# Signs of float64 weights from a leaky rectifier's slope, and weights measured in two groups, in an attention and two-MLP kernel

## The chip, the cores and the metric

One core of one Trainium2 chip runs the whole program. The metric is the device time of one execution in microseconds (us); less is better. TensorE (PE) multiplies, VectorE (DVE) and ScalarE (ACT) prepare its operands and empty PSUM, SyncE (SP) issues the DMAs.

## The reference

```python
x = attention(q, k, v)         # 4 batches, 8 heads, 576 tokens, head size 64, mask in blocks of 64
h = x @ w_in                   # 2304 x 512 times 512 x 2048
x = np.maximum(0.01 * h, h) @ w_out
h = x @ w2_in                  # the second MLP, of the same sizes
return (h * (1.0 / (1.0 + np.exp(-h)))) @ w2_out
```

The weights of both MLPs come as 64-bit floats; q, k and v as 32-bit floats.

## The kernel before

The kernel writes all work down as tasks with a rank and planned costs; a planner (`Schedule.run`) then fixes one order per engine, and on the chip each engine works through its own list and waits at each instruction until its inputs are there. So a change of a cost or a rank reorders everything around it.

The 2304 tokens are cut into six blocks of 384. Block 0's attention comes first. Then the first MLP runs block by block, and its 2048 inner columns in 16 slices, each a step: H (the first product, into the one bank `h`), the gate on ScalarE (leaky rectifier from `h` to `g`), `ghi` (ScalarE) and `glo` (VectorE), its two 16-bit halves, and A (the second product, into `acc` and `u`). PE's list is H of a step, A of the step before, H of the next step, so a gate has an A's time to free `h`. Block 0 multiplies in 32 bits (lines 1763 and 1789), blocks 1 to 5 with two 16-bit halves of x, of the gate and of the weights (lines 1768 to 1770 and 1797). The attention of block n + 1 is laid among the steps of block n: scores `s<-k,q` (lines 1369 and 1462) go into two PSUM banks, the row maximum is DVE's, exp (`p`, line 1480) ACT's, the halves of p ACT's and DVE's (1494, 1499); a DMA transposes them and PE weighs v with them (1312).

The weights are made in three stages.

- `convert` turns 64-bit floats into 32-bit ones, 128x512 at a time: 32 tiles of the first MLP while block 0 is at work, 32 of the second later. Line 441 loads `raw` (three buffers). Line 449 (ACT) scales the upper word as if it were a 32-bit float, so that three zero bits stand ahead. Line 461 (DVE, or 457 on ACT) puts the three low bits that belong to the number into the lower half of a word of `cc`; line 466 (DVE) puts the sign bit into its upper half. Line 479 (DVE) shifts the scaled word left by three, which drops its sign, and joins it with `cc`.
- `measure_weights` (line 530, ACT) and `range_of_weights` find one power of two for all 32 tiles: a maximum, a DMA transpose across partitions (559) and small DVE instructions (550 to 579).
- `split_weights` makes each tile's two 16-bit halves: high (line 614, ACT) and low (line 619, DVE). Block 1's step needs those of its slice.

The gate of blocks 1 to 5 (line 1826) scales by the constant `DOWN`; `w_back` brings the output of a block back. The second MLP works on pairs of blocks in 32 bits (2044 to 2046), then in 16 bits (2223), with sums of products on DVE (2069 to 2080).

Of the kernel before, what the change touches and what calls it, by code (L numbers as in the profile page):

```python
# [7 lines left out]
F32 = mybir.dt.float32  # L8
# [55 lines left out]
V_SLOTS = ((16, 17, 18, 19), (20, 21, 25, 26))  # L64
SPLIT_LEAD, W_RANK, VB_LEAD = 55.0, 0.4, 4.0

# [178 lines left out]
def attn_mlp_mlp(  # L245
# [183 lines left out]

    def convert(src, f, sl, rk, load_rank, to=None, slow=0, lag=0, joint=False, free=()):  # L430

        d = {}
        raw_free, raw_after, raw_users = raws.next()
        cy_free, cy_after, cy_users = cys.next()
        cc_free, cc_after, cc_users = ccs.next()

        def load():
            r = raw_room().bitcast(I64)  # L440
            nc.sync.dma_start(out=r, in_=src[f, :, sl])
            d["r"] = r.bitcast(F32)
            d["w0"] = r.bitcast(U32).rearrange("p (n two) -> p n two", two=2)[:, :, 0]
            d["sign"] = r.bitcast(U16).rearrange("p (n four) -> p n four", four=4)[:, :, 3]
# [6 lines left out]
        def half_words(i):  # L451
            return d["c"].bitcast(U16).rearrange("p (n two) -> p n two", two=2)[:, :, i]

        def low(e):
            d["c"] = cc_room(U32)
            if e == "ACT" and joint:
                nc.scalar.activation(half_words(0), d["w0"], AF.Copy, scale=LOW, bias=-0.5)
            elif e == "ACT":
                nc.scalar.activation(half_words(0), d["w0"], AF.Copy, scale=2.0**-29)
            elif joint:  # L460
                nc.vector.tensor_scalar(half_words(0), d["w0"], 2.0**-29, -0.50001, op0=ALU.mult, op1=ALU.add)
            else:
                nc.vector.tensor_scalar(half_words(0), d["w0"], 2.0**-29, None, op0=ALU.mult)
# [4 lines left out]
        def shifted(e):  # L468
            yu = d["y"].bitcast(U32)
            nc.vector.tensor_scalar(yu, yu, 3, None, op0=ALU.logical_shift_left)  # L470

        def added(e):
            ci = d["c"].bitcast(I32)
            d["x"] = d["c"].bitcast(F32) if to is None else to()
            engine[e].tensor_tensor(d["x"].bitcast(I32), d["y"].bitcast(I32), ci, op=ALU.add)
# [15 lines left out]
        if joint:  # L491
            t_x = plan.add({"DVE": dve(DM)}, [t_y, t_w, t_c, *free], rk, joined)
        else:
            t_t = plan.add({"DVE": dve2x(DM) + 60}, [t_y], rk, shifted)
            t_x = plan.add({"DVE": dve(DM) + 70}, [t_w, t_c, t_t], rk, added)
        raw_users += [t_y, t_w, t_c]
# [14 lines left out]
    def first_weights():  # L511

        got = []
        for i in range(2 * NF):
            f, sl = i // 2, slice((i % 2) * DM, (i % 2 + 1) * DM)
            rk = CONV0 + CONV1 * f
            to = lambda f=f, sl=sl: wx[f][:, sl]
            got.append(convert(w1, f, sl, rk, LOAD0 + RAW0 + 20 * i if i < 4 else rk - CONV_LOAD, to, slow=LATER if i < 4 else 0, joint=True))
        return got

    def measure_weights():

        t_zero = plan.add({"POOL": 150}, [], -100, lambda e: nc.gpsimd.memset(w_sums, V_LEAST))
        tasks = []
        for i, (d, t_x, _) in enumerate(w1_got):
            at = i % 2 * (2 * NF + 1) + i // 2

            def sized(e, d=d, at=at):
                if e == "ACT":
                    nc.scalar.activation(  # L530
                        w_junk, d["x"], AF.Square, scale=SQUARE, accum_out=w_sums[:, at : at + 1]
                    )
                else:
                    nc.vector.tensor_reduce(
                        w_sums[:, at + NF : at + NF + 1], d["x"], axis=AX.X, op=ALU.max, apply_absolute_value=True
                    )

            tasks.append(plan.add({"ACT": act(DM) + 200, "DVE": dve(DM)}, [t_x, t_zero], CONV0 + CONV1 * (i // 2) + W_RANK, sized))
        return tasks

    def range_of_weights():

        sums = w_sums.rearrange("p (s f) -> p s f", s=2)
        top, half, mult, back = (w_small[:, 2 * i : 2 * i + 2] for i in range(4))
        tops = w_tops.rearrange("p (s q) -> p s q", s=2)
        rk = -100.0

        def squared(e):
            m = sums[:, :, NF : 2 * NF]
            nc.vector.scalar_tensor_tensor(m, m, 4 * SQUARE**2, m, op0=ALU.mult, op1=ALU.mult)  # L550
# [27 lines left out]
        def both_back(e):  # L578
            nc.vector.scalar_tensor_tensor(
                w_back, back[:, 0:1], 1.0 / DOWN, back[:, 1:2], op0=ALU.mult, op1=ALU.mult  # L580
            )

        t = plan.add({"DVE": 190}, measure_weights(), rk, squared)
        t = plan.add({"DVE": 200}, [t], rk, most)
        ts = [plan.add({"ACT": act(P), "DVE": 170}, [t], rk, lambda e, s=s: spread(e, s)) for s in (0, 1)]
        t = dma(ts, -1000.0, 80640, turned, 1200, lag=PT_LAG)
        t = plan.add({"DVE": dve(2 * P) + 90}, [t], rk, topped)
        t_half = plan.add({"DVE": 160}, [t], rk, halved)
# [3 lines left out]
        w1_range.update(mult=mult, t_mult=t_mult, t_back=plan.add({"DVE": 160}, [t], 0, both_back))  # L592

    w1_range = {}

    def split_weights():
# [3 lines left out]
        for i in range(2 * NF):  # L600
            f, side = i // 2, i % 2
            sl = slice(side * DM, (side + 1) * DM)
            d, t_x, _ = w1_got[i]
            by = w1_range["mult"][:, side : side + 1]

# [16 lines left out]

            deps = [t_x, w1_range["t_mult"]]
            if f in slot_of("xw"):
# [111 lines left out]
    def first_pair(p):  # L736

        rk = unit3(0, p) - W2_AHEAD
        d0, t0, users0 = convert(w2, 2 * p, slice(0, DM), rk, rk - CONV_LOAD, lag=LAG, joint=True)
        d1, t1, users1 = convert(w2, 2 * p + 1, slice(0, DM), rk, rk - CONV_LOAD, lag=LAG, joint=True)  # L740
        t_free, t_after, t_users = cys.next()
# [33 lines left out]
    def last_raw(p, rk):  # L775
# [5 lines left out]
            convert(  # L781
                w2, 2 * p + i, slice(DM, 2 * DM), rk, rk - CONV_LOAD / 4, room[i], lag=LAG, joint=True, free=busy
            ) for i in (0, 1)
# [1028 lines left out]
    def add_step(blk, f):  # L1812
# [35 lines left out]
        free = older.g_users if older else []  # L1848
        s.t_gate1 = plan.add({"ACT": act(n, True)}, [s.t_g1, *free], GATE + rk, gate1)
        s.g_users = []  # L1850
# [585 lines left out]
```

## Time and profile before

| | |
|---|---|
| time, median of 3 runs | 891.86 us (891.21 to 892.37) |
| the profiled execution | 891.37 us |
| its span, first to last instruction | 889.6 us |
| busy: PE, DVE, ACT | 866.6, 765.1, 633.7 us |
| mean granted clock of PE | 0.993 of 2.4 GHz |

A row of the profile gives a line of the kernel, the engine, the operation and its tiles (out<-in, buffer numbers left out); x is the number of instructions. Idle time stands with its releaser, the instruction whose end let the waiting one go.

### The profile page before, as it was taken

Reading aid. Unit: us, or ns where it says so; the run is one execution under the profiler, and the core shown is the slowest. Engines: PE = TensorE matmul, PEld = TensorE weight load, DVE = VectorE, ACT = ScalarE, POOL = GpSimd, SP = SyncE. Lnnn points to the kernel's source line nnn. Section 1 sums busy time; section 2 is a strip of 40 time slices with the busy share of each in tenths; the row PEclk is TensorE's granted clock in tenths of the full one; section 3 lists DMA queues with packets and bytes.
Section 4 is the critical chain, followed back from the end, with each engine's and each line's share of the span. In section 5 each row is a group of like instructions: output and inputs, shape, how many; then the busy total and the mean of one; then the engine's idle time right before and its main releaser. Section 6 shows DMA issues by size and latency. Waiting matters only on the chain.

```text
span 889.6 us, 18360 instructions
## 1 busy us (share of the span) xinstructions
PE 866.6 (97%) x6569; PEld 650.4 (73%) x6569; DVE 765.1 (86%) x1730; ACT 633.7 (71%) x1455; POOL 15.3 (2%) x75
## 2 busy tenths in 40 slices
PE   9899999998999999999999999999999989999997
PEld 4555556665676666666666668999999978888886
DVE  6888889999988998788847679989897999999976
ACT  6989889886776677677646468988797985444432
POOL 0000000000000000000000000000000000000000
PEclk9999999998999999999999999999999999999999
DMA  8579838765668589655535226588868874553531
GB/s 288 180 212 221 233 105 216 185 132 131 166 150 164 133 172 196 150 144 113 110 65 185 93 71 227 195 289 267 277 205 269 287 253 141 157 163 121 165 108 60
DMA packets 179179, 155.71 MB, mean 175 GB/s; under 512 B 108304, under 2 KB 155152, under 8 KB 179088
## 3 DMA queue, kind: packets, MB, share of 16 engines
q1 hardware_dynamic: 179088, 154.54, 62.2%
q8 instruction: 51, 0.84, 0.4%
q14 instruction: 40, 0.33, 0.1%
HBM read 93.85 MB, written 35.65 MB: 146 GB/s over the span
## 4 chain that ended last, share of the span: by engine, by line
PE 68%; DVE 9%; ACT 4%; DMA 2%; issue 2%; SPq 0%; DVEq 0%; POOL 0%; ACTq 0%; POOLq 0%
PE acc L1797 11%; PE acc L2223 7%; PE h L1768 5%; PE h L1770 5%; PE h L1769 5%; PE s L2223 5%; PE s L1462 4%; PE u L1797 4%; PE x L1312 2%; PE u L2223 2%; PE x L2223 2%; PE acc L2045 2%; PE acc L2044 2%; PE acc L2046 2%; PE s L2044 1%
## 5 line engine op out<-in xcount | busy, mean ns | idle before, releaser
L1797 PEld LDWEIGHTS <-w 128*128 128x128 f16 x840 | 78.6, 98 | 54.6 <-issue 4.4
L1797 PE MATMUL acc<-ghi,w 128*128 128x384 f16 x420 | 103.1, 328 | 0.8 <-ACT cc L1901 0.8
L1768 PE MATMUL h<-h,w 128*128 128x384 f16 x280 | 92.6, 331 | 0.8 <-DVE w L619 0.8
L1769 PE MATMUL h<-l,w 128*128 128x384 f16 x280 | 92.1, 329 | 0.0
L1770 PE MATMUL h<-h,w 128*128 128x384 f16 x280 | 92.1, 329 | 0.0
L1480 ACT ACTIVATE p<-s,st 128x288 f32<-128x288 f32 (+4 forms) x120 | 62.4, 521 | 40.1 <-DVE st L1472 24.7
L1462 PE MATMUL s<-k,q 128*128 128x288 f32 (+5 forms) x288 | 77.5, 364 | 5.3 <-ACT p L1480 5.1
L1826 ACT ACTIVATE g<-h 128x384 f32<-128x384 f32 x80 | 39.1, 489 | 48.6 <-PE h L1770 47.9
L412 DVE TENSOR_TENSOR glo<-g,ghi 128x384 f16<-128x384 f32 x80 | 44.3, 554 | 28.9 <-ACT ghi L401 28.0
L1797 PE MATMUL acc<-glo,w 128*128 128x384 f16 x210 | 68.5, 326 | 0.0
L1494 ACT ACTIVATE hl<-p,st 128x576 f16<-128x576 f32 (+5 forms) x90 | 55.0, 626 | 17.9 <-issue 6.7
L1499 DVE SCALAR_TENSOR_TENSOR hl<-p,st,hl 128x576 f16<-128x576 f32 (+4 forms) x96 | 58.8, 625 | 3.3 <-ACT hl L1494 2.8
L1462 PEld LDWEIGHTS s<-k,q 128*128 128x128 f32 x288 | 46.9, 190 | 18.6 <-ACT p L1480 8.7
L2223 PEld LDWEIGHTS <-y 128*128 128x128 f16 x525 | 51.8, 99 | 10.6 <-issue 3.0
L2223 PEld LDWEIGHTS <-x 128*128 128x128 f16 x492 | 48.3, 98 | 6.1 <-issue 0.3
L2105 ACT ACTIVATE h<-e 128x384 f32<-128x384 f32 x96 | 46.9, 489 | 1.8
L2096 ACT ACTIVATE e<-e 128x384 f32<-128x384 f32 (+1 forms) x72 | 42.2, 621 | 6.0 <-DVE e L2076 6.0
L449 ACT ACTIVATE cy<-raw 128x512 f32<-128x512 f32 x64 | 42.5, 667 | 3.1 <-DMA raw<-w 2.9
L1768 PEld LDWEIGHTS <-w 128*128 128x128 f16 x280 | 27.5, 98 | 21.7 <-issue 3.1
L401 ACT ACTIVATE ghi<-g 128x384 f16<-128x384 f32 x77 | 40.2, 522 | 1.4
L1770 PEld LDWEIGHTS <-w 128*128 128x128 f16 x280 | 27.6, 99 | 18.5 <-issue 0.7
L1769 PEld LDWEIGHTS <-w 128*128 128x128 f16 x280 | 27.7, 99 | 15.4 <-issue 0.7
(347 smaller groups left out, 2367.6 us busy)
## 6 DMA issues: line engine op xcount, KB each, us to landing
raw<-w SPq DMA_DIRECT2D x64, 512.0 KB, 4.8
raw<-g SPq DMA_DIRECT2D x64, 256.0 KB, 3.2
g<-e SPq DMA_DIRECT2D x48, 192.0 KB, 3.4
g<-e SPq DMA_DIRECT2D x24, 384.0 KB, 2.9
kqr<-kq_l SPq DMA_DIRECT2D x16, 480.0 KB, 3.7
kqr<-kq_l SPq DMA_DIRECT2D x16, 416.0 KB, 3.4
y<-yT SPq DMA_DIRECT2D x12, 384.0 KB, 4.7
l<-w2k SPq DMA_DIRECT2D x18, 256.0 KB, 4.3
```

Of the source, the lines that this page charges most:

```text
L412: engine[e].tensor_tensor(lo, x, hi, op=ALU.subtract)
L449: nc.scalar.activation(d["y"], d["top"], AF.Copy, scale=2.0**-112)
L1462: nc.tensor.matmul(s[:, :w], hd.q[:, a : a + P], hd.k[:, k0:k1], start=i + j == 0, stop=i == len(hds) - 1 and j == 1,)
L1480: nc.scalar.activation(p[:rows, k0:k1], u.s[piece][:rows, :w], AF.Exp, bias=nm[:rows], accum_out=s2[:rows, piece : piece + 1])
L1494: nc.scalar.activation(hl[:rows, 0, :n], p[:rows], AF.Copy, scale=rc[:rows])
L1499: nc.vector.scalar_tensor_tensor(hl[:rows, 1, :n], p[:rows], rc[:rows], hl[:rows, 0, :n], op0=ALU.mult, op1=ALU.subtract)
L1768: nc.tensor.matmul(h, w1_lo[s.f][:, sl], hi[:, c, : s.n], start=c == 0, stop=False)
L1769: nc.tensor.matmul(h, w1_hi[s.f][:, sl], lo[:, c, : s.n], start=False, stop=False)
L1770: nc.tensor.matmul(h, w1_hi[s.f][:, sl], hi[:, c, : s.n], start=False, stop=c == NC - 1)
L1797: nc.tensor.matmul(s.acc[c][:, : s.n], a, b, start=s.f == 0 and i == 0, stop=s.f == NF - 1 and i == 2)
L2105: nc.scalar.activation(h_all[:, :n], out_()[:, at : at + n], AF.Square, scale=SQUARE, accum_out=sum_at(col))
L2223: nc.tensor.matmul(o, a[:, x], b, start=i == 0 and j == 0 and q == 0, stop=i == NP - 1 and q == 2, skip_group_check=True,)
```

## The change

The weights' conversion no longer has a sign instruction: line 449 becomes a leaky rectifier with slope 2^32 for negative numbers, whose larger exponent becomes the sign bit when line 479 shifts left by three. The low bits become a full 32-bit word: a shift on DVE, or a scaled copy on ACT.

The weights are measured, scaled and split in two groups, slices 0 to 5 and 6 to 15, each with a power of two of its own. The gate's constant scale becomes a column of `w_downs`, one number per partition, that makes up for the group's power of two. Four planning numbers move: conversions rank earlier (CONV0), measuring earlier (W_RANK), the attention of blocks 2 to 5 earlier (ATT), and splits 11 steps later (SPLIT_LEAD), which puts them behind whatever else is ready.

```diff
-CONV0, CONV1, CONV_LOAD = 10.5, 0.7, 78.0
-ATT0, ATT1, ATT, ATT_SLOPE, AHEAD, V_LATE = 11.0, 0.3, 54.0, 0.8, 7.5, 0.0
+CONV0, CONV1, CONV_LOAD = 9.0, 0.7, 78.0
+ATT0, ATT1, ATT, ATT_SLOPE, AHEAD, V_LATE = 11.0, 0.3, 44.0, 0.8, 7.5, 0.0
-SPLIT_LEAD, W_RANK, VB_LEAD = 55.0, 0.4, 4.0
+W_GROUPS = ((0, 6), (6, 16))
+SPLIT_LEAD, W_RANK, VB_LEAD = 66.0, -3.0, 4.0
...
         def scaled(e):
             d["y"] = cy.tile([P, DM], F32, tag="cy", name="cy")
-            nc.scalar.activation(d["y"], d["top"], AF.Copy, scale=2.0**-112)
+            nc.scalar.activation(d["y"], d["top"], AF.Prelu, alpha=2.0**32, scale=2.0**-112)
...
-                nc.vector.tensor_scalar(half_words(0), d["w0"], 2.0**-29, -0.50001, op0=ALU.mult, op1=ALU.add)
+                nc.vector.tensor_scalar(d["c"], d["w0"], 29, None, op0=ALU.logical_shift_right)
-        def signed(e):
-            nc.vector.tensor_scalar(half_words(1), d["sign"], 0x8000, None, op0=ALU.bitwise_and)
...
-        t_c = plan.add({"DVE": dve2x(DM) + 110}, [t_load], rk, signed, [t_w])
+        t_x = plan.add({"DVE": dve(DM)}, [t_y, t_w, *free], rk, joined)
+        raw_users += [t_y, t_w]
...
+        n = len(W_GROUPS)
+        for g in range(n):
+            range_of_group(g)
+        most, factor = w_small[:, 8 * n : 8 * n + 1], w_small[:, 8 * n + 1 : 8 * n + 2]
+        def largest(e):
+            nc.vector.tensor_reduce(most, w_backs, axis=AX.X, op=ALU.max)
+        def inverse(e):
+            nc.vector.tensor_scalar(factor.bitcast(I32), most.bitcast(I32), EXPONENT, None, op0=ALU.bitwise_xor)
+        def downs(e):
+            nc.vector.tensor_scalar(w_downs, w_backs, factor, 0.5 * DOWN, op0=ALU.mult, op1=ALU.mult)
+        def whole_back(e):
+            nc.vector.tensor_scalar(w_back, most, 1.0 / DOWN, None, op0=ALU.mult)
...
-                nc.scalar.activation(s.g, s.h[:, :n], AF.Prelu, alpha=LEAK, scale=DOWN)
+                at = group_of(f)
+                nc.scalar.activation(s.g, s.h[:, :n], AF.Prelu, alpha=LEAK, scale=w_downs[:, at : at + 1])
```

On DVE, in block 0, the conversion of two tiles stands before as follows (479 joins, 466 makes the sign, 461 the low bits, 1380 and 1381 belong to the attention).

```order
L479 SCALAR_TENSOR_TENSOR x<-cy,cc 128x512
L466 TENSOR_SCALAR cc<-raw 128x512
L461 TENSOR_SCALAR cc<-raw 128x512
L479 SCALAR_TENSOR_TENSOR x<-cy,cc 128x512
L466 TENSOR_SCALAR cc<-raw 128x512
L1380 TENSOR_SCALAR st<-st 128x2
L1381 RECIPROCAL st<-st 128x2
L479 SCALAR_TENSOR_TENSOR x<-cy,cc 128x512
```

The same place in the changed kernel (456 makes the low bits, 460 joins, 1408 is the attention's low half of p):

```order
L1390 TENSOR_REDUCE st<-s 128x1
L1408 SCALAR_TENSOR_TENSOR hl<-p,st,hl 128x256
L456 TENSOR_SCALAR cc<-raw 128x512 x2
L1408 SCALAR_TENSOR_TENSOR hl<-p,st,hl 128x256
L460 SCALAR_TENSOR_TENSOR x<-cy,cc 128x512 x2
L456 TENSOR_SCALAR cc<-raw 128x512
```

Two instructions of DVE per tile are left of three.

On DVE, between `glo` of slices 13 and 14 of block 1, the list before still holds low halves of the weights of slices 14 and 15 (`w_1727`, `w_1750`), between the attention's instructions:

```order
L412 TENSOR_TENSOR glo<-g,ghi 128x384
L619 SCALAR_TENSOR_TENSOR w_1727<-l,wm,w_1727 128x512
L1470 MEMSET s 64x64
L1472 TENSOR_REDUCE st<-s 128x1
L1499 SCALAR_TENSOR_TENSOR hl<-p,st,hl 128x576
L1474 TENSOR_REDUCE st<-s 128x1
L619 SCALAR_TENSOR_TENSOR w_1727<-l,wm,w_1727 128x512
L619 SCALAR_TENSOR_TENSOR w_1750<-l,wm,w_1750 128x512
```

In the changed kernel none is left behind slice 9's gate; the list between `glo` of slices 10 and 11 is:

```order
L413 TENSOR_TENSOR glo<-g,ghi 128x384
L1516 SCALAR_TENSOR_TENSOR hl<-p,st,hl 128x576
L1516 SCALAR_TENSOR_TENSOR hl<-p,st,hl 128x320
L1516 SCALAR_TENSOR_TENSOR hl<-p,st,hl 128x448
L1504 TENSOR_TENSOR st<-st 128x1
L1506 TENSOR_SCALAR st<-st 128x1
L1507 RECIPROCAL st<-st 128x1
L1487 MEMSET s 64x64
L1489 TENSOR_REDUCE st<-s 128x1
L413 TENSOR_TENSOR glo<-g,ghi 128x384
```

The splits have moved ahead: before, 8 of the 32 low halves stand ahead of block 1's first `glo` and 24 behind; now 21 and 11. Of the high halves on ACT, 10 stand ahead of block 1's first gate before and 27 now.

On PE, before, between A of block 1's slice 11 (`w_1549`) and H of slice 13 (`w_1657`) five pairs of scores and 72 products with v stand with no layer step among them:

```order
L1797 MATMUL u<-glo,w_1549 128x384
L1462 MATMUL s<-k,q 128x320 x2
L1462 MATMUL s<-k,q 128x448 x2
L1312 LDWEIGHTS vp
...
L1312 MATMUL x<-raw,vp 64x128
L1462 MATMUL s<-k,q 128x288 x4
L1312 LDWEIGHTS vp
...
L1462 MATMUL s<-k,q 128x512 x2
L1768 LDWEIGHTS w_1657
L1768 MATMUL h<-h_242,w_1657 128x384
```

In the changed kernel there, around H of slice 12 (`w_1385`), each pair of scores has products of a step or of v on either side:

```order
L1479 MATMUL s<-k,q 128x320 x2
L1814 LDWEIGHTS xw
L1814 MATMUL acc<-ghi,xw 128x384
...
L1329 MATMUL x<-raw,vp 64x128
L1479 MATMUL s<-k,q 128x448 x2
L1785 LDWEIGHTS w_1385
L1785 MATMUL h<-h_243,w_1385 128x384
...
L1787 MATMUL h<-h_243,w_1385 128x384
L1479 MATMUL s<-k,q 128x288 x2
L1785 LDWEIGHTS w_1385
```

The pairs of scores have been drawn apart; the number of PE's matmuls is the same in both kernels. Both kernels load ACT's function tables twice.

## Rows read from the trace of the kernel before

**Rows 1.** The page: busy time, and PE in 40 equal slices.

```profile
PE 866.6 (97%) x6569; PEld 650.4 (73%) x6569; DVE 765.1 (86%) x1730; ACT 633.7 (71%) x1455; POOL 15.3 (2%) x75
PE   9899999998999999999999999999999989999997
```

**Rows 2.** Stages: busy us per engine, PEclk, DMA share, GB/s.

```profile
40.00:140.00 100.00, 98.25 (x466) 57.04 (x465) 86.65 (x249) 87.04 (x223) 0.76 (x4) 1.00 0.72 192
140.00:198.00 58.00, 57.95 (x469) 36.49 (x469) 56.38 (x142) 50.43 (x114) 4.60 (x19) 1.00 0.79 180
198.00:205.00 7.00, 4.65 (x83) 3.05 (x81) 6.65 (x22) 5.30 (x15) 0.20 (x1) 0.98 0.44 102
205.00:212.00 7.00, 5.67 (x18) 2.66 (x19) 6.03 (x15) 3.29 (x10) 0.41 (x2) 0.53 0.75 150
```

**Rows 3.** What PE waited for: us in total, times, longest us.

```profile
PE s L1462 <- ACT p L1480: 5.1, 6, 1.7
PE s L2223 <- DVE e L2069: 2.7, 1, 2.7
```

**Rows 4.** Timeline of PE in the burst and just behind it.

```profile
205.51 1.22 PE L1462 MATMUL s<-k,q 128*128 128x512 f32 x2 [1.51 <-ACT p L1480]
207.55 0.50 PE L1768 MATMUL h<-h,w 128*128 128x384 f16 x1 [0.82 <-DVE w L619]
207.84 0.53 PE L1769 MATMUL h<-l,w 128*128 128x384 f16 x1
208.16 0.53 PE L1770 MATMUL h<-h,w 128*128 128x384 f16 x1
...
214.94 0.33 PE L1769 MATMUL h<-l,w 128*128 128x384 f16 x1
215.10 0.33 PE L1770 MATMUL h<-h,w 128*128 128x384 f16 x1
```

**Rows 5.** Timeline of PE at the end of block 0.

```profile
123.59 0.56 PE L1462 MATMUL s<-k,q 128*128 128x320 f32 x2 [1.75 <-ACT p L1480]
```

**Rows 6.** Groups of DVE: busy us, mean ns of one, idle before.

```profile
L466 DVE TENSOR_SCALAR cc<-raw 128x512 uint16<-128x512 uint16 x64 | 28.9, 455 | 0.0
L461 DVE TENSOR_SCALAR cc<-raw 128x512 uint16<-128x512 uint32 x47 | 21.5, 457 | 2.6 <-DMA raw<-w 2.4
L479 DVE SCALAR_TENSOR_TENSOR l<-cy,cc 128x512 uint32<-128x512 uint32 x20 | 13.7, 684 | 1.8 <-ACT cy L449 1.5
```

**Rows 7.** Groups of ACT, with the same columns.

```profile
L449 ACT ACTIVATE cy<-raw 128x512 f32<-128x512 f32 x64 | 42.5, 667 | 3.1 <-DMA raw<-w 2.9
L1826 ACT ACTIVATE g<-h 128x384 f32<-128x384 f32 x80 | 39.1, 489 | 48.6 <-PE h L1770 47.9
L401 ACT ACTIVATE s<-x 128x384 f32<-128x384 f32 x20 | 9.7, 486 | 12.6 <-PE x L2046 12.5
L1901 ACT ACTIVATE cc<-acc,yb 128x384 f32<-128x384 f32 x6 | 3.5, 578 | 2.3 <-DVE y L1903 1.4 <-PE acc L1797 0.9
```

**Rows 8.** The weights' instructions: ns min/median/max, first and last start in us.

```profile
L614 ACT ACTIVATE w<-w,wm x6: 728/736/748, 149.9 to 160.8; 128x512 f16<-128x512 f32 x6
L619 DVE SCALAR_TENSOR_TENSOR w<-w,wm,w x6: 731/738/747, 175.9 to 208.3; 128x512 f16<-128x512 f32 x6
L576 DVE TENSOR_SCALAR wm<-wm x1: 160/160/160, 129.3 to 129.3; 128x2 f32<-128x2 f32 x1
```

**Rows 9.** What SP's queue waited for in the first 150 us.

```profile
SPq L441 <- DVE cc L466: 29.5, 12, 10.7
```

**Rows 10.** The chain that ended last, where the second MLP starts and changes stage: start, us.

```profile
534.53 0.72 DVE cc L466 x2
...
716.35 0.88 DVE e L2069
```

**Rows 11.** Timelines of ACT and PE in a step without attention.

```profile
499.78 0.49 ACT L1826 ACTIVATE g<-h 128x384 f32<-128x384 f32 x1 [0.96 <-PE h L1770]
...
501.53 0.33 PE L1768 MATMUL h<-h,w 128*128 128x384 f16 x1
```

More of the change, by code (lines that the diff above doesn't have):

```diff
@@ L428, in attn_mlp_mlp, with convert @@
     raws, cys, ccs = Turns(RAWS), Turns(CYS), Turns(CCS)
[L430 removed]
+    def convert(src, f, sl, rk, load_rank, to=None, slow=0, lag=0, free=()):
         d = {}
@@ L448, in scaled @@
             d["y"] = cy.tile([P, DM], F32, tag="cy", name="cy")
-            nc.scalar.activation(d["y"], d["top"], AF.Copy, scale=2.0**-112)
-        def half_words(i):
-            return d["c"].bitcast(U16).rearrange("p (n two) -> p n two", two=2)[:, :, i]
+            nc.scalar.activation(d["y"], d["top"], AF.Prelu, alpha=2.0**32, scale=2.0**-112)
         def low(e):
             d["c"] = cc_room(U32)
[L456 to L460, printed above, removed]
-                nc.vector.tensor_scalar(half_words(0), d["w0"], 2.0**-29, -0.50001, op0=ALU.mult, op1=ALU.add)
-            else:
-                nc.vector.tensor_scalar(half_words(0), d["w0"], 2.0**-29, None, op0=ALU.mult)
-        def signed(e):
-            nc.vector.tensor_scalar(half_words(1), d["sign"], 0x8000, None, op0=ALU.bitwise_and)
[L468 to L475, printed above, removed]
+            if e == "ACT":
+                nc.scalar.activation(d["c"], d["w0"], AF.Copy, scale=LOW, bias=-0.5)
+            else:
+                nc.vector.tensor_scalar(d["c"], d["w0"], 29, None, op0=ALU.logical_shift_right)
         def joined(e):
@@ new lines, in sums_of, with measure_weights, sized @@
+    def sums_of(g):
+        a, b = W_GROUPS[g]
+        at = 2 * (2 * a + g)
+        return w_sums[:, at : at + 2 * (2 * (b - a) + 1)].rearrange("p (s f) -> p s f", s=2)
+    def measure_weights(g):
+        a, b = W_GROUPS[g]
+        tasks = []
+        for i in range(2 * a, 2 * b):
+            d, t_x, _ = w1_got[i]
+            sums = sums_of(g)[:, i % 2]
+            one, other = (sums[:, at : at + 1] for at in (i // 2 - a, i // 2 - a + b - a))
+            def sized(e, d=d, one=one, other=other):
@@ L539, in measure_weights @@
-        return tasks
-    def range_of_weights():
-        sums = w_sums.rearrange("p (s f) -> p s f", s=2)
-        top, half, mult, back = (w_small[:, 2 * i : 2 * i + 2] for i in range(4))
+                    nc.scalar.activation(w_junk, d["x"], AF.Square, scale=SQUARE, accum_out=one)
+                else:
+                    nc.vector.tensor_reduce(other, d["x"], axis=AX.X, op=ALU.max, apply_absolute_value=True)
+            tasks.append(plan.add({"ACT": act(DM) + 200, "DVE": dve(DM)}, [t_x, w1_range["zero"]], CONV0 + CONV1 * (i // 2) + W_RANK, sized))
@@ L545, in range_of_weights, with range_of_group @@
+        return tasks
+    def range_of_group(g):
+        a, b = W_GROUPS[g]
+        sums, small = sums_of(g), w_small[:, 8 * g : 8 * g + 8]
+        top, half, mult, back = (small[:, 2 * i : 2 * i + 2] for i in range(4))
         tops = w_tops.rearrange("p (s q) -> p s q", s=2)
+        before = w1_range.get(g - 1)
         rk = -100.0
         def squared(e):
-            m = sums[:, :, NF : 2 * NF]
+            m = sums[:, :, b - a : 2 * (b - a)]
             nc.vector.scalar_tensor_tensor(m, m, 4 * SQUARE**2, m, op0=ALU.mult, op1=ALU.mult)
@@ L579, in both_back @@
             nc.vector.scalar_tensor_tensor(
-                w_back, back[:, 0:1], 1.0 / DOWN, back[:, 1:2], op0=ALU.mult, op1=ALU.mult
+                w_backs[:, g : g + 1], back[:, 0:1], 1.0, back[:, 1:2], op0=ALU.mult, op1=ALU.mult
             )
-        t = plan.add({"DVE": 190}, measure_weights(), rk, squared)
+        t = plan.add({"DVE": 190}, measure_weights(g), rk, squared)
         t = plan.add({"DVE": 200}, [t], rk, most)
[L585 to L588, printed above, removed]
+        free = [before["turn"]] if before else []
+        ts = [plan.add({"ACT": act(P), "DVE": 170}, [t, *free], rk, lambda e, s=s: spread(e, s)) for s in (0, 1)]
+        free = [before["topped"]] if before else []
+        t_turn = dma([*ts, *free], -1000.0, 80640, turned, 1200, lag=PT_LAG)
+        t_top = plan.add({"DVE": dve(2 * P) + 90}, [t_turn], rk, topped)
+        t_half = plan.add({"DVE": 160}, [t_top], rk, halved)
         t = plan.add({"DVE": 130}, [t_half], rk, inverted)
@@ L591, in range_of_weights @@
         t = plan.add({"DVE": 130}, [t_half], 0, turned_back)
-        w1_range.update(mult=mult, t_mult=t_mult, t_back=plan.add({"DVE": 160}, [t], 0, both_back))
+        t = plan.add({"DVE": 160}, [t], 0, both_back)
+        w1_range[g] = {"mult": mult, "t_mult": t_mult, "turn": t_turn, "topped": t_top, "back": t}
+    def range_of_weights():
+        w1_range["zero"] = plan.add({"POOL": 150}, [], -100, lambda e: nc.gpsimd.memset(w_sums, V_LEAST))
+        n = len(W_GROUPS)
[10 more added lines that the diff above has]
+            nc.vector.tensor_scalar(w_back, most, 1.0 / DOWN, None, op0=ALU.mult)
+        t_most = plan.add({"DVE": 160}, [w1_range[g]["back"] for g in range(n)], 0, largest)
+        t = plan.add({"DVE": 130}, [t_most], 0, inverse)
+        w1_range["downs"] = plan.add({"DVE": 160}, [t], 0, downs)
+        w1_range["t_back"] = plan.add({"DVE": 130}, [t_most], 0, whole_back)
     w1_range = {}
@@ L603, in split_weights @@
             d, t_x, _ = w1_got[i]
-            by = w1_range["mult"][:, side : side + 1]
+            one = w1_range[group_of(f)]
+            by = one["mult"][:, side : side + 1]
             def parts(f=f, sl=sl):
@@ L621, in low @@
                 )
-            deps = [t_x, w1_range["t_mult"]]
+            deps = [t_x, one["t_mult"]]
             if f in slot_of("xw"):
@@ L781, in last_raw @@
             convert(
-                w2, 2 * p + i, slice(DM, 2 * DM), rk, rk - CONV_LOAD / 4, room[i], lag=LAG, joint=True, free=busy
+                w2, 2 * p + i, slice(DM, 2 * DM), rk, rk - CONV_LOAD / 4, room[i], lag=LAG, free=busy
             ) for i in (0, 1)
@@ L1848, in add_step @@
         free = older.g_users if older else []
-        s.t_gate1 = plan.add({"ACT": act(n, True)}, [s.t_g1, *free], GATE + rk, gate1)
+        s.t_gate1 = plan.add(
+            {"ACT": act(n, True, min(blk, 1))}, [s.t_g1, *free, *([w1_range["downs"]] if blk else [])], GATE + rk, gate1
+        )
         s.g_users = []
```

35 lines of the change are left out of this document (10 added, 25 removed).

## The prediction

> **What bounds the kernel now.** I read the busy line of the page first. PE is busy for 866.6 of a span of 889.6 us, DVE for 765.1, ACT for 633.7 [rows 1]. So 23 us of PE's time are idle, and since the change leaves the number of PE's matmuls as it is, those 23 us and the stretches of lower clock are all that it can win. Next come the 40 slices of PE: each is 22.2 us, and besides the last only three fall under 90%: the second (22 to 44 us), the tenth (200 to 222 us) and the thirty-third (711 to 734 us) [rows 1]. The windows show what these are. From 40 to 140 us, while block 0 runs and the weights are converted, PE is busy for 98.25 of 100 us, DVE for 86.65 and ACT for 87.04; from 140 to 198 us PE idles for 0.05 us. Then come 198 to 205 us with PE busy for 4.65 of 7 us, and 205 to 212 us with 5.67 of 7 and a granted clock of 0.53 [rows 2]. The waits name the partners: PE's scores wait for ACT's exp `p`, 6 times and 5.1 us in all, and one wait of 2.7 us on DVE's `e` stands in the second MLP [rows 3]. The timeline shows one place for most of this: a pair of scores that starts at 205.51 after a wait of 1.51 us, the layer's first product at 207.55 after 0.82 us on DVE's low half of a weight [rows 4]; and one wait of 1.75 us on `p` at 123.59 [rows 5].
>
> The tenth slice is a burst. PE's list holds five pairs of scores and the products with v between A of slice 11 and H of slice 13, with no layer step among them. Scores have two banks, each freed by an exp, so PE goes at ACT's and DVE's pace there, while DVE, busy for 6.65 of the first 7 us [rows 2], still has low halves of weights between the attention's instructions: the last ones run at 208.3 us [rows 8].
>
> **The change part by part.**
>
> *The sign instruction goes.* 64 times 455 ns are 28.9 us of DVE [rows 6]. PE waits for DVE in few of the places where it stood. In block 0 (32 of the 64, 14.6 us) PE has 1.75 us idle in 100 [rows 2], so nearly all of it is work that PE covers; it buys room on DVE, which the splits then use. SP's queue waited 29.5 us, 12 times, for the sign instruction to free a `raw` buffer [rows 9]; now the low bits or the scaled copy free it. That starts loads earlier, but DMA has 0.72 to 0.79 of its time taken there and PE does not wait for these loads, so I take 0.
>
> *The scaled copy becomes a leaky rectifier.* The gate is one with 128x384 at 489 ns, and a plain copy of the same size from PSUM takes 486 [rows 7]: the function costs nothing. 64 copies stay at 667 ns.
>
> *The low bits as a 32-bit shift.* No row has this instruction. Its bounds are 455 to 457 ns (one source, 16-bit output) and 684 ns (two sources, 32-bit output) [rows 6]. It has one source, so I take 457; the other end costs 0.23 us for each of the 52 that DVE now has, 27 of them ahead of block 1: 6.2 us there. On this the Trainium skill, "VectorE: DVE Perf Modes", section "What auto-detection actually checks", says that what counts is the kind of operand and the even layout, with all in SBUF: by it a single-source instruction on 32-bit words still has the faster mode. No run shown has the case; by the page the term would be the lower end.
>
> *The gate's scale from a column.* An ACT instruction with a per-partition operand of the same size took 578 ns against 486 for one without [rows 7]: 92 ns more, and 80 gates make 7.4 us of ACT. PE's next H needs `h` free, and has an A's time for that: a gate that starts at 499.78 ends at 500.27, H starts at 501.53 [rows 11]. 1.26 us of cover against 0.09, so 0; without the cover it would be the whole 7.4.
>
> *Two groups.* A second range chain is some 14 small DVE instructions at 160 ns or less [rows 8], 2.2 us, ahead of block 1, plus a DMA. All splits of slices 0 to 5 can start when 12 of the 32 tiles are measured. I count what now stands ahead of block 1's first step. On DVE: 32 signs go (−14.6), 13 more low halves of splits at 738 ns (+9.6), 2 high halves and 2 more low bits (+2.4), the range (+2.2), and some attention (+4): about +4 us net. On ACT: 17 more high halves at 736 ns (+12.5), a measurement and two low bits fewer (−2), attention that has moved behind (−5): about +5 us. Idle there are 13.35 us of DVE and 12.96 us of ACT in 40 to 140 us [rows 2]. So it fits, with 8 to 9 us left on each; but these engines' idle time lies where it lies, and new small waits of PE are to be expected. Nothing prices them but the row that they resemble, 1.75 us once [rows 5]; I put +1.0 us, from 0 to 1.75 times four for the bad case.
>
> *What the packing gives back.* The gain lies behind, in the steps of block 1: 13 low halves fewer (9.6 us of DVE) and 17 high ones fewer on ACT, and the scores drawn apart. The terms, with bounds:
> - The burst: 2.35 us idle from 198 to 205, 1.33 from 205 to 212 [rows 2], and the low clock. Behind it the layer's products start 0.32 us apart (207.84, 208.16), while at full clock it is 0.16 (214.94, 215.10) [rows 4]; of the 18 in the window some 12 are such, 1.9 us. The pair with 512 columns took 1.22 us [rows 4], where 0.56 for 320 columns [rows 5] makes 0.90: 0.3. Together 5.9; bounds 0 and 5.9. In the new list each pair of scores has layer products or products with v beside it, which cover its exp. I take 5.0, because a pair or two will still wait.
> - The end of block 0, 1.75 us [rows 5]: 0 to 1.75, take 0.9, since its `p` stands behind work of ACT that is now different.
> - The start of the second MLP: the chain goes through two signs, 0.72 us [rows 10]: 0 to 0.72, take 0.5.
> - The second MLP's change of stage: PE waits 2.7 us for `e` [rows 3], which the chain has on DVE [rows 10]. DVE's list there is the same but for one small instruction that moves ahead; signs are long done. 0 to 2.7, take 0.4.
> - The start, 22 to 44 us, where the slice shows 80 to 89% [rows 1], 2.2 to 4.4 us idle: measurements come earlier and compete on ACT, a sign less on DVE. From −1.5 to +1.5, take 0.
>
> Sum: −5.0 − 0.9 − 0.5 − 0.4 + 1.0 = −5.8 us against the profiled execution's 891.37: 885.6. The median of the runs is 0.5 above that execution, so 886.0.
>
> **The rivals.**
>
> *A, more than that.* Every named wait goes: 5.9 + 1.75 + 0.7 + 2.7 = 11.1 us, and no new one comes: 880.8. Against it: the wait in the second MLP has nothing to do with what is changed.
>
> *B, the change does not show.* PE is at 97% and the relief of DVE and ACT falls where PE covers it; the attention of the next blocks, which ranks earlier, forms its burst at another place. Then only the 0.5 to 1 us of the second MLP's start and of block 0's end is left: 890.5 to 892. For it: the attention of a block needs the same exps in the same 16 steps. Against it: from 140 to 198 us PE idles for 0.05 us in 58 with the same kind of work between the steps [rows 2], so spread work does hide.
>
> *C, slower.* The splits and the second range are packed into block 0. If the shift takes 684 ns, DVE's room of 13.35 us [rows 2] shrinks by 4 + 6.2 to 3 us, and exp's maxima and the halves of `p` come late; PE's scores then wait as they do at 205.51. Its price is that burst's, 5.9 us each time, clock included. It decides when the new waits exceed the gains and the 1.8 us of measurement: 5.0 + 0.9 + 0.5 + 0.4 + 1.8 = 8.6 us, so one burst and two waits as in [rows 5] do (5.9 + 3.5 = 9.4): 891.86 − 6.8 + 9.4 = 894.5; two bursts, 11.8, make 896.9. The row behind the burst shows what waiting costs twice: a granted clock of 0.53 from 205 to 212 us [rows 2], after a stretch with PE at 4.65 of 7. The Trainium skill, "TensorE: Matmul & The Clock Gate", section "HAM oscillation — how this bites in real kernels", describes this: an engine that is starved again and again loses its clock and pays for each stall a second time. By that, with this row, packed work that starves PE in several places would cost more than its idle time; the trace agrees for this one burst.
>
> **How the numbers follow.** The forecast (883.5 to 888.5, that is the burst gone wholly or by two thirds) has 0.55; A 0.10; B 0.18; C 0.17. A change of 0.2%, 1.8 us, is about what can be told from no change, so 890.1 to 893.6 is "same". Faster: 0.55 + 0.10 + 0.05 of B = 0.70; same 0.13; slower 0.17. The range leaves out most of C and half of A: 880.5 to 893.5.
>
> **What would show it.** In the profile after: no DVE instruction with a 16-bit output of the sign; the shift at about 457 ns, if 684 then C's condition is there; the gate at about 580 ns with H's start unmoved; the copy with the rectifier at 667. PE's tenth slice at 9, windows at 195 to 215 us with PE over 95% and a clock of 1.0; waits of scores on `p` down from 5.1 us to under 2; DVE's busy time down by some 25 us and ACT's up by 4 to 8. The steps of the second MLP shift by the same 5 us and the wait on `e` stays near 2.7. I would be wrong if the windows from 40 to 140 us show more than 3 us of idle PE, or if another window with a low clock stands where the earlier attention now ranks, in the later half of blocks 1 to 4.

## The result, and the profile after

The changed kernel takes 877.38 us, the median of four runs (876.53 to 878.52), against 891.54 for the kernel before: a ratio of 0.9844, with an interval of 0.9826 to 0.9863, that is 12 to 16 us less. The forecast was 886.0, its range 880.5 to 893.5: the direction is right, the size is not. The profiled execution after took 878.52 us, the longest of the four, with a span of 876.8, 12.8 us under that of before.

The page after, its busy line and the 40 slices of PE and of its clock:

```profile
PE 860.7 (98%) x6569; PEld 648.6 (74%) x6569; DVE 751.4 (86%) x1700; ACT 623.8 (71%) x1434; POOL 14.9 (2%) x75
...
PE   8899999999999999999999999999999999999997
...
PEclk9999999999999999999999999999999999999999
```

The tenth slice and the thirty-third, which stood at 8 in [rows 1], are at 9; the start has become no better. PE's idle time fell from 23.0 to 16.1 us, and its busy time by 5.9 us with the same number of matmuls. The windows of [rows 2], after:

```profile
40.00:140.00 100.00, 99.84 (x475) 57.79 (x474) 91.92 (x255) 91.58 (x228) 0.76 (x4) 1.00 0.77 208
140.00:198.00 58.00, 57.69 (x515) 36.81 (x515) 55.52 (x154) 42.31 (x105) 4.34 (x20) 1.00 0.72 154
198.00:205.00 7.00, 7.00 (x59) 4.37 (x54) 6.66 (x19) 6.26 (x15) 0.20 (x1) 1.00 0.74 156
205.00:212.00 7.00, 7.00 (x75) 4.57 (x74) 6.83 (x17) 3.80 (x9) 0.20 (x1) 1.00 0.76 178
```

Block 0 is fuller, by 5.3 us on DVE and 4.5 on ACT, and PE idles for 0.16 us there in place of 1.75. The burst is gone, and the clock of 0.53 with it. All that PE waits for from 40 to 300 us after (us in total, times, longest):

```profile
PE s L1479 <- ACT p L1497: 0.2, 1, 0.2
PE s L1386 <- ACT p L1394: 0.2, 1, 0.2
```

The new instructions, as groups of DVE and ACT, and the first high and the last low halves of weights (ns min/median/max, first and last start in us):

```profile
L456 DVE TENSOR_SCALAR cc<-raw 128x512 uint32<-128x512 uint32 x52 | 21.2, 421 | 4.5 <-DMA raw<-w 4.1
L1844 ACT ACTIVATE g<-h,wd 128x384 f32<-128x384 f32 x80 | 46.1, 577 | 46.9 <-PE h L1787 46.2 <-DVE l L1264 0.6
L449 ACT ACTIVATE cy<-raw 128x512 f32<-128x512 f32 x64 | 42.2, 666 | 2.6 <-DMA raw<-w 2.0 <-DVE w L413 0.5
...
L629 ACT ACTIVATE w<-y,wm x4: 707/711/732, 64.8 to 88.1; 128x512 f16<-128x512 f32 x4
L634 DVE SCALAR_TENSOR_TENSOR w<-l,wm,w x4: 733/743/744, 154.8 to 183.8; 128x512 f16<-128x512 f32 x4
```

The same two groups before:

```profile
L614 ACT ACTIVATE w<-y,wm x6: 705/706/722, 129.6 to 133.1; 128x512 f16<-128x512 f32 x6
...
L619 DVE SCALAR_TENSOR_TENSOR w<-l,wm,w x4: 731/745/747, 214.0 to 218.4; 128x512 f16<-128x512 f32 x4
```

Splitting now begins at 64.8 us in place of 129.6, while later tiles are still converted, and its last low half starts at 183.8 us in place of 218.4. (The prediction read 208.3 us as the last one before; that row [rows 8] is one of several groups of low halves, and this one is later.)

Where the time went is read from the start of the same instruction in both timelines:

| reached | before, us | after, us | gained since the line above |
|---|---|---|---|
| first gate of block 0 | 38.70 | 38.28 | 0.4 |
| last gate of block 0 | 132.71 | 129.85 | 2.4 |
| first gate of block 3 | 312.49 | 300.79 | 8.8 |
| last gate of block 5 | 530.98 | 519.56 | −0.3 |
| last product of the second MLP's first layer | 713.22 | 701.81 | 0.0 |
| last product of all | 884.11 | 871.27 | 1.4 |

The largest step, from the last gate of block 0 to the first of block 3, as windows between these gates, before and after:

```profile
132.71:312.49 179.78, 174.80 (x1515) 112.45 (x1515) 167.86 (x455) 137.81 (x338) 8.44 (x38) 0.98 0.70 160
129.85:300.79 170.94, 170.53 (x1514) 111.09 (x1513) 156.94 (x438) 127.10 (x315) 7.55 (x36) 1.00 0.68 150
```

With one matmul more or less, PE's idle time falls from 5.0 to 0.4 us there and its busy time by 4.3 us.

Two signs that the prediction named did not come. DVE's busy time fell by 13.7 us where some 25 were forecast, and ACT's fell by 9.9 where 4 to 8 more were forecast. In its new order the planner gave DVE copies, high halves and two measurements that ACT had before, and ACT makes 12 tiles' low bits in place of 17.

### The profile page after: what moved, and what is told of

It reads as the page before. It is cut to its first block, busy times and chain, and to the rows that moved or that the text cites. A ratio compares the mean times of both kernels' runs of the same rounds, so it can differ in the third digit from the quotient of the medians.

```text
span 876.8 us, 18274 instructions
## 1 busy us (share of the span) xinstructions
PE 860.7 (98%) x6569; PEld 648.6 (74%) x6569; DVE 751.4 (86%) x1700; ACT 623.8 (71%) x1434; POOL 14.9 (2%) x75
## 4 chain that ended last, share of the span: by engine, by line
PE 79%; DVE 9%; ACT 6%; DMA 3%; issue 2%; DVEq 0%; POOL 0%; ACTq 0%; POOLq 0%; SPq 0%
PE acc L1814 11%; PE acc L2243 7%; PE h L1785 5%; PE h L1787 5%; PE h L1786 5%; PE s L2243 5%; PE s L1479 4%; PE u L1814 4%; PE h L1780 3%; PE x L1329 3%; DMA raw<-w 3%; PE u L2243 2%; PE acc L2065 2%; PE acc L2066 2%; PE acc L2064 2%; PE x L2243 2%
## 5 line engine op out<-in xcount | busy, mean ns | idle before, releaser
L1785 PE MATMUL h<-h,w 128*128 128x384 f16 x280 | 91.9, 328 | 0.0
L1844 ACT ACTIVATE g<-h,wd 128x384 f32<-128x384 f32 x80 | 46.1, 577 | 46.9 <-PE h L1787 46.2
L1479 PEld LDWEIGHTS s<-k,q 128*128 128x128 f32 x288 | 47.0, 189 | 11.8 <-ACT p L1497 2.8
```

The lines of the kernel that those rows point to most:

```text
L1479: nc.tensor.matmul(s[:, :w], hd.q[:, a : a + P], hd.k[:, k0:k1], start=i + j == 0, stop=i == len(hds) - 1 and j == 1,)
L1785: nc.tensor.matmul(h, w1_lo[s.f][:, sl], hi[:, c, : s.n], start=c == 0, stop=False)
```

## The experiments

**Which of the three parts.** Signs, groups and planning numbers were put in one by one and in pairs. Each time the planner made an order of its own. The edits:

```diff
 s_alone: convert as in the change, nothing else
-            nc.vector.tensor_scalar(half_words(1), d["sign"], 0x8000, None, op0=ALU.bitwise_and)
 g_alone: measuring, range, split and gate as in the change, convert and numbers as before
+W_GROUPS = ((0, 6), (6, 16))
 n_alone: the four numbers
+CONV0, CONV1, CONV_LOAD = 9.0, 0.7, 78.0
+ATT0, ATT1, ATT, ATT_SLOPE, AHEAD, V_LATE = 11.0, 0.3, 44.0, 0.8, 7.5, 0.0
+SPLIT_LEAD, W_RANK, VB_LEAD = 66.0, -3.0, 4.0
```

> The kernel before with the new conversion alone (leaky rectifier, 32-bit low bits, no sign instruction); one group and the old planning numbers. Theory R (relief: DVE without 28.9 us of signs can make the low halves of the weights earlier, and the burst of scores at 198 to 212 us goes with its low clock): 880 to 884 us, 15 of 32 low halves ahead of block 1's first gate half, PE idle at the end of block 1 under 2 us. Theory W (two groups: the splits come ahead because the range of slices 0 to 5 is known early): 888 to 892, the burst stays, since a run of 10 scores is still in PE's list. Theory N (the planning numbers draw the scores apart): 888 to 892 as well.

> The kernel before with two groups and the gate's scale from a column alone; signs as before, old planning numbers. Theory R: 889 to 893, since DVE has the 28.9 us of signs and 2 us more. Theory W: 881 to 885. Theory N: 889 to 893. The gate takes 578 ns in all of them, and costs nothing.

> The kernel before with the four planning numbers of the change alone; signs and one group as before. Theory R: 890 to 896, nothing relieved and two runs of 6 and 8 scores in PE's list. Theory W: the same. Theory N (attention ranked 10 steps earlier draws the scores apart): 880 to 885.

> The changed kernel with the four old planning numbers: no signs, two groups. Theory R: 876 to 881, no run of six or more scores in PE's list, 21 low halves ahead. Theory W: 876 to 882 too. Theory N: 886 to 891, since without the numbers the burst stays.

> The kernel before with the new conversion and the four new planning numbers, one group of weights and the constant scale of the gate. s_alone is at 885.9, the changed kernel at 877.4. If the two groups matter because all low halves come ahead of slice 9 (theory W'), this one, with 19 of 32 low halves ahead of block 1 but a range that waits for all 32 tiles, stays at 884 to 888, with PE idle between 198 and 240 us. If the numbers alone close the rest (theory N'), it is at 877 to 880.

> The changed kernel with the old conversion: 64 sign instructions of 455 ns on DVE, 16-bit low bits. PE's list has a run of 22 scores with 72 products with v. Theory R (nothing goes without the relief of DVE): 898 to 905, worse than g_alone's 892.4, since the numbers alone were at 901.0. Theory N' (the numbers help once there are two groups): 880 to 886.

Medians in us, with the interval of the ratio to the kernel before (890.8 in these runs, 891.5 beside the change):

| | old numbers | new numbers |
|---|---|---|
| signs, one group | before | 901.0 (1.0091 to 1.0122) |
| signs, two groups | 892.4 (1.0007 to 1.0033) | 902.3 (1.0122 to 1.0149) |
| no signs, one group | 885.9 (0.9932 to 0.9968) | 885.7 (0.9939 to 0.9964) |
| no signs, two groups | 880.6 (0.9869 to 0.9898) | 877.4 (0.9826 to 0.9863) |

No part does it alone. Without the signs 4.9 us go, two groups alone cost 1.6, both together gain 10.2: 6.8 more than their sum. The planning numbers cost 10 us where the signs are, nothing with one group and no signs, and bring 3 with both. Theory N, that the planning numbers draw the scores apart, falls, and theory W as it was put (two groups alone at 881 to 885) does too. Theory R named the right sizes for g_alone and sg_old_numbers, but s_alone came out 2 us short of it and n_alone 5 over its 896; in the last two runs, theory W' (two groups are needed besides) and theory R are borne out at 885.7 and 902.3.

Where the single parts lose is seen in PE's timelines. Two groups with signs, g_alone, then no signs with one group, s_alone, then the numbers alone:

```profile
197.57 1.16 PE L1504 MATMUL s<-k,q 128*128 128x320 f32 x4 [2.43 <-ACT p L1522]
...
216.35 0.50 PE L1810 MATMUL h<-h,w 128*128 128x384 f16 x1 [2.60 <-DVE w L659]
```

```profile
219.85 0.69 PE L1437 MATMUL s<-k,q 128*128 128x192 f32 x4 [1.87 <-ACT p L1455]
221.17 1.19 PE L1437 MATMUL s<-k,q 128*128 128x512 f32 x2 [0.63 <-DVE k L412]
```

```profile
192.07 0.85 PE L1462 MATMUL s<-k,q 128*128 128x288 f32 x2 [3.26 <-ACT p L1480]
...
213.50 0.50 PE L1768 MATMUL h<-h,w 128*128 128x384 f16 x1 [8.02 <-DVE vs L1156]
```

With two groups but signs, DVE is late with low halves (11 of 32 ahead of block 1, and PE waits 2.60 us for one of them). Without signs but with one group, 15 are ahead and no such wait is left, but the run of ten scores still stands in PE's list, three slices later. With the planning numbers alone, PE waits 8 us where DVE is at work for the next block's v (line 1156), ahead of what PE needs.

**The signs, with the order kept.** Two kernels take the planner out of the question. One is the kernel before, in its own order, with the new conversion and the sign instruction left out; the other the changed kernel, in its own order, with an instruction of that size put back.

```diff
 no_sign_order_kept (the kernel before; y and low bits as in the change)
         def signed(e):
-            nc.vector.tensor_scalar(half_words(1), d["sign"], 0x8000, None, op0=ALU.bitwise_and)
+            pass
 sign_back_same_order (the changed kernel)
         def joined(e):
+            words = d["y"].bitcast(U16).rearrange("p (n two) -> p n two", two=2)[:, :, 1]
+            nc.vector.tensor_scalar(words, words, 0, None, op0=ALU.bitwise_or)
```

> The kernel before with the new conversion, but every instruction left in the order of before: the sign instruction is only left out of DVE's list (64 times 455 ns), one group, old numbers. If PE covered the signs where they stood, as the prediction took it, the gain is that of the few places where PE waits behind one: 889 to 890.5, with the burst at 198 to 212 us and its clock as before. If DVE's time ahead of block 1 decides by itself, 883 to 886, as s_alone's 885.9.

> The changed kernel with one more DVE instruction ahead of each join: an OR with 0 on the upper 16-bit words of the scaled tile, in place, 64 times, of the size of the old sign instruction (455 ns, 29 us in all); the planned order is that of the changed kernel. Theory T (DVE's time itself counts): the waits come back, 884 to 890. Theory O (the lighter conversion acts only through the order that the planner can make with it, since DVE has slack while the weights are converted): 877 to 880; the 32 in block 0 are 14.6 us, DVE's room in 40 to 140 us is about 8, so up to 3 us may show at block 0's end.

In the order of before, leaving out 64 signs gains 1.8 us: 889.1 (0.9972 to 0.9992). In the changed order, putting them back costs 14.3 us: 891.7 (1.0002 to 1.0021 of the kernel before). Windows of no_sign_order_kept, and a row of its timeline:

```profile
40.00:140.00 100.00, 98.93 (x473) 57.44 (x472) 78.39 (x220) 86.78 (x224) 0.76 (x4) 1.00 0.71 195
198.00:205.00 7.00, 3.87 (x64) 2.42 (x58) 6.64 (x21) 5.32 (x14) 0.36 (x2) 0.87 0.70 147
```

```profile
203.25 1.22 PE L1462 MATMUL s<-k,q 128*128 128x512 f32 x2 [1.51 <-ACT p L1480]
```

DVE has 8.3 us more room in block 0 and PE idles 0.7 us less there and starts the burst some 2 us earlier; the wait of 1.51 us is that of [rows 4]. And sign_back_same_order: its windows (the second from the last gate of block 0 to the first of block 3), the group of the added instruction, and PE's waits from 40 to 140 us:

```profile
40.00:140.00 100.00, 94.77 (x435) 54.00 (x436) 95.44 (x262) 83.24 (x212) 1.08 (x4) 1.00 0.74 201
139.62:310.38 170.76, 169.80 (x1510) 110.44 (x1509) 157.05 (x438) 126.99 (x316) 7.55 (x36) 1.00 0.67 150
530.00:700.00 170.00, 165.53 (x942) 161.37 (x941) 152.93 (x272) 140.84 (x346) 0.00 (x0) 1.00 0.74 245
```

```profile
L461 DVE TENSOR_SCALAR cy<-cy 128x512 uint16<-128x512 uint16 x64 | 29.0, 454 | 8.5 <-ACT cy L449 8.5
```

```profile
PE s L1388 <- ACT p L1396: 3.9, 5, 1.4
PE h L1782 <- ACT g L1848: 1.1, 2, 0.8
PE s L1481 <- ACT p L1396: 1.0, 1, 1.0
```

With DVE at 95.4 of 100 us, scores wait for exp again and again and PE loses 5.2 us in that window; the last gate of block 0 comes at 139.62 us, 9.8 later than in the changed kernel. Another 3.4 us go in the first layer of the second MLP. Between the two, from block 0's last gate to block 3's first, it takes 170.8 us, as the changed kernel does (170.9), where the kernel before took 179.8. None of the added instructions stands there (they run from 14 to 118 and from 475 to 673 us), and DVE has 157.1 us of work, as in the changed kernel (156.9), where it had 167.9 before. So the order's gain in blocks 1 and 2 stays, and the time put back is paid where it stands. Theory T (884 to 890) named the direction, but 891.7 lies over its range, and the waits are not those of before, when block 0's last gate stood at 132.71. Theory O's 877 to 880 holds only for the order of before. Instructions of the same size are worth 1.8 us in one order and 14 in the other. (The OR stands behind ACT's scaled copy, where the sign needed only the raw words, so 14.3 is taken as an upper end for the signs themselves.)

**The low halves in the burst.** The first suspect for the burst was DVE's load from low halves of weights at the start of block 1.

```diff
 cheap_lows_order_kept (the kernel before, the last 24 of 32 low halves)
-                nc.vector.scalar_tensor_tensor(parts()[1], d["x"], by, parts()[0], op0=ALU.mult, op1=ALU.subtract)
+                nc.vector.tensor_scalar(parts()[1], d["x"], by, 2.0**-12, op0=ALU.mult, op1=ALU.mult)
 cheap_lows_new_order: the same, and planned with
+                t_lo = plan.add({"DVE": dve2x(DM, 1)}, [t_hi], rk, low)
```

> The kernel before in its own order, with the last 24 of the 32 low halves of the weights made by a single-source instruction (the scaled weight times a constant, not the remainder; it doesn't wait for the high half), some 400 ns in place of 738 by estimate, so about 8 us less of DVE at the start of block 1. What is left out is the exact low half of these weights. Theory D (the burst is paid because DVE is still at low halves there): 884 to 887, most of the 6.5 us of the burst gone and its clock at 1. Theory L (the burst is paid because ten scores stand side by side and two banks pace them by exp): 889.5 to 891, only the wait of 0.82 us on a low half gone.

> The kernel before with the last 24 low halves made by a single-source instruction (480 ns in place of 740; the exact low half is left out), and the order made anew with that cost; signs, one group and old numbers as before. If DVE's load from low halves in block 1 is what bunches the scores and costs: 881 to 885. If it is the late range or the bunching itself (a run of 12 scores is still in PE's list, three steps later): 886 to 890, with the burst moved to 215 to 235 us.

With the order kept 888.4 (0.9959 to 0.9988), with a new order 888.8 (0.9970 to 0.9998). The group, a window and the timeline of the first, and a row of the second's timeline:

```profile
L624 DVE TENSOR_SCALAR w<-w,wm 128x512 f16<-128x512 f32 x6 | 2.9, 480 | 0.0
```

```profile
205.00:212.00 7.00, 7.00 (x28) 3.81 (x27) 4.83 (x10) 3.12 (x8) 0.20 (x1) 0.63 0.66 122
```

```profile
202.93 0.92 PE L1465 MATMUL s<-k,q 128*128 128x512 f32 x2 [1.51 <-ACT p L1483]
204.71 0.50 PE L1771 MATMUL h<-h,w 128*128 128x384 f16 x1 [0.85 <-DVE w L624]
```

```profile
221.91 1.17 PE L1465 MATMUL s<-k,q 128*128 128x128 f32 x4 [2.84 <-ACT p L1483]
```

Theory D falls. With a third less time per low half, the wait of 1.51 us is there to the hundredth, with a clock of 0.63 behind it. (888.4 lies between the ranges of theories D and L.) With a new order the burst moves to 222 us, as expected by the other theory.

Is it the bunch of scores alone that costs? Three windows go from the first score of a run of ten to the next product of a step. They are from the kernel before, cheap_lows_order_kept and sn_one_group:

```profile
198.65:207.55 8.90, 5.47 (x82) 3.54 (x83) 8.43 (x29) 7.21 (x20) 0.41 (x2) 0.84 0.63 138
```

```profile
196.40:204.71 8.31, 5.14 (x85) 3.37 (x83) 7.85 (x29) 6.82 (x19) 0.57 (x2) 0.92 0.69 148
```

```profile
213.63:216.78 3.15, 2.97 (x44) 2.22 (x40) 1.69 (x6) 1.46 (x4) 0.21 (x1) 1.00 0.78 186
```

It is not. In the first two, DVE is busy for some 95% of the run, with one low half of a weight in each: nearly all the rest is the attention's work. In sn_one_group DVE has 1.69 us of work in the run, and PE passes its ten scores in 3.15 us with 0.2 us idle and a clock of 1.00. So the bunch was dear where the attention's other work on DVE and ACT fell together with it. That compares kernels whose whole orders differ; no edit moved this work alone.

**The gate's scale.**

```diff
-                nc.scalar.activation(s.g, s.h[:, :n], AF.Prelu, alpha=LEAK, scale=w_downs[:, at : at + 1])
+                nc.scalar.activation(s.g, s.h[:, :n], AF.Prelu, alpha=LEAK, scale=DOWN)
```

> The changed kernel with the gate scaled by a constant again in place of the column (the second group's factor is left out), same order otherwise. The gate takes 489 ns in place of 577, 7 us less of ACT. If the column costs nothing, as predicted: 877.4, within 1 us. If ACT's time in block 1 to 5 decides something: 875 or less.

877.75 (877.27 to 881.08) against 877.38: the 7 us of ACT are hidden.

**Neighbours of the change.** Five kernels move one to three numbers of the changed kernel.

```diff
 sg_conv_rank: old numbers but CONV0 = 9.0        conv_rank_8, conv_rank_8_5: CONV0 = 8.0, 8.5
 groups_4_and_12: W_GROUPS = ((0, 4), (4, 16))    old_att_and_lead: ATT = 54.0, SPLIT_LEAD = 55.0
```

> No signs, two groups, and of the planning numbers only the earlier conversions (CONV0 9.0). sg_old_numbers was at 880.6, the changed kernel at 877.4. If this number is what closes the 3 us: 877 to 878.5. If it is the other two: 880 to 883, as two runs of eight scores are in PE's list here.

> The changed kernel with conversions ranked earlier still (CONV0 8.0): no run of six or more scores in PE's list (the changed kernel has one), but 18 low halves ahead of block 1 in place of 21. If runs of scores are what costs: 875.5 to 877. If low halves ahead of block 1 are: 878 to 881.

> The changed kernel with conversions ranked half a step earlier (CONV0 8.5): 22 low halves ahead of block 1, two runs of six scores. conv_rank_8 was at 884.9. If earlier conversion crowds block 0: 879 to 884; if not: 876 to 878.

> The changed kernel with the groups' border at slice 4 in place of 6. The first range is known four tiles earlier. If an earlier first range is what helps: 875 to 877. If the number of low halves ahead of block 1 is (17 in place of 21), or the runs of eight scores in blocks 3 and 4: 878 to 882.

> The changed kernel with two of the four planning numbers put back (ATT 54, SPLIT_LEAD 55), so that only conversions and measuring rank earlier. ATT alone changes nothing in the list of any engine once signs are gone. If earlier conversions and measuring make the last 3 us: 877 to 878.5. If splits that are ranked behind all else make it: 880 to 882.

881.8, 884.9, 880.9, 883.4 and 882.7 us. All lie under the kernel before by 6 to 10 us, and over the change by 3.5 to 7.5. Three lie outside every range that was expected: 884.9, 883.4 and 882.7. Neither count explains their sequence: conv_rank_8 has no run of six scores behind block 1's first product and is the slowest; conv_rank_8_5 and old_att_and_lead have 22 low halves ahead of block 1, one more than the change, and are 3.5 and 5.3 us slower. By its expectation, old_att_and_lead differs from the change through its SPLIT_LEAD, since ATT alone changes no engine's list; no run has ATT by itself. In the profiled executions the differences arise ahead of the last gate of block 5: from there to the last product each takes 351.9 to 352.0 us, as the changed kernel does.

## Why the prediction missed

- **Signs covered by PE.** Right, for the order of before: 1.8 us for all 64; in the profiled executions, 2.6 us apart, 1.5 of it is there at the first gate of block 0 (37.15 us), 0.7 more at its last, and none comes in the second MLP. The prediction also said that their room is what the splits use. In the new order that room is needed: in sign_back_same_order the gain as a whole is gone. It is lost in block 0 and in the second MLP, where the instructions stand, while the 8.8 us of blocks 1 and 2 stay: there DVE has 11 us less to do than before, since the splits have moved ahead into that room.
- **The shift at 457 ns.** It took 421, so the condition of rival C (684) never came up. The Trainium skill, "VectorE: DVE Perf Modes", section "What auto-detection actually checks", put it at the lower end, and the trace agrees: 421 against 684 for the two-source join of the same words.
- **Copy, gate, cover.** 666 ns and 577 ns, nothing on PE's path; right, by constant_gate_scale.
- **The burst, 5.0 of 5.9, and new waits of +1.0.** This is the step that failed, in size. Between the end of block 0 and the end of block 5 the kernel gained 8.6 us, where 4.0 were forecast. The upper bound of 5.9 was itself too low. It held 3.7 us of PE's idle time and 2.2 for the low clock; from block 0's last gate to block 3's first, idle time fell by 4.6 and busy time by 4.3. The bound ended at 212 us, but two waits behind the burst went with it, which the timeline of before has as

```profile
226.49 0.69 PE L1462 MATMUL s<-k,q 128*128 128x192 f32 x4 [0.49 <-ACT p L1480]
...
234.29 0.48 PE L1797 MATMUL acc<-ghi,w 128*128 128x384 f16 x2 [0.76 <-ACT cc L1901]
```

  With them the idle time is accounted for. The 2.1 us of busy time beyond the term for the clock are not assigned to a row. And the new waits, put at +1.0, came to 0.4 us from 40 to 300 us.
- **The end of block 0, −0.9.** −2.4. Between the first and the last gate of block 0 PE's idle time fell from 2.3 to 0.7 us, with the wait of 1.75 us [rows 5] gone; the other 0.8 is work that moved on, 430 matmuls in place of 437.
- **The start, 0; the second MLP's start, −0.5; its change of stage, −0.4.** −0.4, 0.0 and −1.4. The wait on `e` fell from 2.7 [rows 3] to 1.4 us. It stayed at 1.4 with the signs put back and was 2.4 in no_sign_order_kept, so it goes with the order of that stretch. But waits on the halves of the operands beside it grew, so PE's idle time behind the first layer fell by only 0.4 us; its busy time fell by 1.1. Before, and after:

```profile
PE s L2223 <- DVE y L700: 0.9, 1, 0.9
717.00:721.00 4.00, 3.73 (x22) 2.73 (x22) 3.73 (x6) 3.97 (x11) 0.00 (x0) 0.60 0.59 208
```

```profile
PE s L2243 <- DVE e L2089: 1.4, 1, 1.4
PE s L2243 <- DVE y L715: 1.2, 1, 1.2
PE s L2243 <- DVE x L715: 0.5, 1, 0.5
705.60:709.60 4.00, 3.81 (x36) 3.27 (x34) 3.79 (x6) 4.00 (x9) 0.00 (x0) 1.00 0.71 227
```

  Behind the long wait the kernel before had a second stretch of low clock, 0.60 from 717 to 721 us, for which the prediction had no term; after, the same place keeps 1.00.

  The sum is −12.8 against −5.8. Of the 7.0 us between them about 4.2 lie inside the bounds, in terms that were taken below their upper end for caution, each by itself, and 3.4 lie beyond the upper ends: 2.7 behind block 0 and 0.7 at its end. The second MLP's start takes 0.5 back. Rival A, with all terms at the upper end and 880.8, was nearest, and had a chance of 0.10.
- **Rival C** did not come, but a part of its mechanism is real: with DVE at 95.4 of 100 us in block 0 PE idles for 5.2 us there, and at 91.9, where the change stands, for 0.16. The low clock that was part of its price did not follow: it is 1.00 in that window.
- **Rival B**, the burst that only moves, is what s_alone and cheap_lows_new_order did.

What stays open: what makes the planner bunch scores. With no signs, one group has a run of ten (s_alone) and two groups have none of six (sg_old_numbers), but two groups with signs and the new numbers have one of 22 (gn_with_signs); DVE's low halves are not it, by cheap_lows_new_order. Open, too, are the 3.5 to 7.5 us between the change and its neighbours. They belong to this one order, and no edit to a single instruction was found that carries them. No version faster than the change was found.

## What to carry to other kernels

An instruction on an engine with slack can be nearly free where it stands and still be worth ten microseconds, once the order is made anew without it (here 1.8 us with the order kept; in a new one 4.9 with one group and 11.8 with two): cost such an edit twice, in the old order and by the work that can move into the room. Where a list shows that a burst has been drawn apart, take its whole price, with its clock and the waits in its wake: terms that hang on the same condition come together, and shading each by itself shades the sum several times. And where a change moves the numbers of a planner, a part of its gain is one lucky order among neighbours; here that part was a quarter to a half.

## What was not expected of the hardware

A logical shift of 128x512 words on DVE took 421 ns, 36 less than the scaled copy of the same words into 16 bits [rows 6]. And a low granted clock followed the burst in the three profiles with the order of before (0.53, 0.64, 0.63 from 205 to 212 us, behind 2.4 to 3.2 us of idle PE from 198 to 205), while sign_back_same_order, with 5.2 us of idle time from 40 to 140 us in waits of at most 1.4 us each, kept a clock of 1.00.
